# Who makes the low parts of an expert's weights, and where a slot's conversion piece stands

## The chip, the cores and the metric

The kernel runs on one core of a Trainium2 chip. The metric is the device time of one execution in microseconds, lower is better. Three runs of the kernel before gave 1194.30, 1198.21 and 1198.25 us, median 1198.21. The profiled execution took 1196.37 us. Its span, from the first to the last instruction, is 1194.7 us.

TensorE (PE in the views) multiplies matrices, VectorE (DVE), ScalarE (ACT) and GpSimd (POOL) work on elements, SyncE (SP) issues most DMAs.

## What is computed

Three stages stand behind one another. Cut to what matters:

```python
def _moe_ref(x, w_gate, w_output_gate, w1, w2):      # x: 1792 x 768, from attention
    logits = x @ w_gate
    e_idx = np.argmax(logits, axis=1)                # one of 8 experts for each token
    ...
    for e in range(E):
        mask = e_idx == e
        h = np.maximum(x[mask] @ w1[e], 0.0)         # 768 x 1024
        ye = h @ w2[e]                               # 1024 x 768
        out[mask] = gate_w[mask, None] * eom[mask, e, None] * ye

def _moe2_ref(x, w_in, w_out):                       # feed-forward, 768 x 2048 x 768
    h = x @ w_in
    return (h * np.cos(h)) @ w_out
```

Before them an attention with a sigmoid in place of the softmax makes `x` (4 batches, 12 heads, 448 tokens, 64 wide). The feed-forward's weights come as 64-bit floats.

## The kernel before

**High and low parts.** A matmul on full 32-bit floats is done as three matmuls on numbers of a shorter type: each operand is split into a high part (a rounding copy, on ScalarE) and a low part (the number less its high part, on VectorE or GpSimd), and high x high, high x low and low x high are added up in PSUM. The function `split` does this for a piece of weights of 128 x 1536: `w1h` and `w2h` are high parts, `w1l` and `w2l` low parts, four pieces of each for an expert. Its last argument chooses GpSimd for the low part.

**Slots.** The tokens are sorted by expert into slots of 128; here 19 slots (0 to 18) hold tokens. `slot` works on one:

1. `p0`, the left half of the hidden layer: 18 matmuls (`mm1`, lines 242 to 244) with the first two pieces of `w1`. VectorE clips it at zero into `hr` (line 722).
2. `p1`, the right half: 18 matmuls with the last two pieces. After nine of them TensorE turns the left half (`pht`, line 728), ScalarE takes its high part `hh` (line 731), VectorE its low part `hl` (line 732).
3. The next slot's tokens are turned (`xh`, `xl`), and the right half's `hr` is made.
4. The second layer into `py`: eight groups of six matmuls (`mm2`, lines 741 and 742). After the first group the right half is turned; its `hh` and `hl` follow, and seven groups.
5. `scale_y` copies `py`, scaled, to `ysb`, two thirds on ScalarE (line 835) and a third on VectorE (lines 836 and 837), and it is stored.

**A change of expert.** The weights of one expert are in SBUF at a time, and raw weights come into four buffers `rw`. Where slot s+1 has another expert, `split1(s + 1)` at the end of slot s splits the new `w1` and loads the new `w2` into the buffers that this frees. In slot s+1 `split2(0)` to `split2(3)` split `w2` between the slot's own steps, and load the `w1` of the expert after. Which slots have a new expert is known only on the chip, so each split stands in a conditional block on a flag; the engines named in `SPLIT` read the flag. Of `w1l` the fourth piece is GpSimd's; of `w2l` the second is GpSimd's, and of the fourth each of VectorE and GpSimd does half (line 782).

**The conversion piece.** The feed-forward's weights are brought from 64-bit floats to high and low parts in 48 pieces, spread over the whole of the first two stages. `conv_step` does one, and slots 1 to 17 have one each. A piece is: `ctu` on ScalarE, four operations on VectorE, `chi` on ScalarE (which needs VectorE's fourth), a fifth on VectorE, and three on GpSimd (lines 160, 161 and 163). It also stores the piece before and loads the next one.

Each engine works off its instructions in the order in which the code is written; a wait holds up all that stands behind it on that engine.

Of the kernel before, what the change touches and what calls it, by code (L numbers as in the profile page):

```python
# [9 lines left out]
F32 = mybir.dt.float32  # L10
# [5 lines left out]
AF = mybir.ActivationFunctionType  # L16
ALU = mybir.AluOpType
# [3 lines left out]
ENG = mybir.EngineType  # L21
# [3 lines left out]
CONV_EARLY = 40  # L25
# [28 lines left out]
def tile_attn_moe_cos(ctx: ExitStack, tc: tile.TileContext, q, k, v, wg, wog, w1, w2, w_in, w_out, out):  # L54
    nc = tc.nc
# [54 lines left out]
    w1r = [t.rearrange("p (k f) -> p k f", k=3) for t in rw]  # L110
    w2r = [t.rearrange("p (k f) -> p k f", k=2) for t in rw]
# [17 lines left out]
    def conv_load(i):  # L129
        if i >= len(conv_list):  # L130
            return
        which, h, r = conv_list[i]
        raw = craw[i % 2]
        if which == "i":
            src = w_in[r * P : (r + 1) * P, h * CW : (h + 1) * CW].bitcast(U32)
            nc.sync.dma_start(raw.rearrange("p f t -> p (f t)"), src)
        else:
            src = wo_in[h][:, :, r * CO : (r + 1) * CO].bitcast(U32)
            nc.sync.dma_start(raw.rearrange("p (two f) t -> p two (f t)", two=2), src)
# [26 lines left out]
    def conv_store():  # L166
        while conv_out:
            which, h, r, parts_ = conv_out.pop()
            for t, f in enumerate(parts_):
                if which == "i":  # L170
                    c0 = h * CW // P
                    nc.sync.dma_start(
                        wi_d[c0 : c0 + CW // P, :, t, r, :].rearrange("c p f -> p c f"),
                        f.rearrange("p (c f) -> p c f", f=P),
                    )
                else:
                    nc.sync.dma_start(
                        wo_to[h, t][:, :, r * CO : (r + 1) * CO], f.rearrange("p (two f) -> p two f", two=2)
                    )

    conv_at = [0]

    def conv_step(whole=True):
        conv_end()
        conv_store()
        conv_load(conv_at[0] + 1)
        conv_rest.append(conv(conv_at[0]))
        next(conv_rest[0], None)
        conv_at[0] += 1
        if whole:  # L190
            conv_end()
# [3 lines left out]
    def conv_end():  # L195
        while conv_rest:
            next(conv_rest.pop(), None)
# [3 lines left out]
    w1h = [pre.tile([P, 3, 512], F32R, name="w1h0")]  # L201
    w1l = [pre.tile([P, 3, 512], F32R, name="w1l0")]
# [4 lines left out]
    def w1_src_d(e, i):  # L207
        nh, kg = divmod(i, 2)
        return w1[bass.ds(e, 1)].rearrange("o (k p) f -> p (o k) f", p=P)[
            :, 3 * kg : 3 * kg + 3, 512 * nh : 512 * nh + 512  # L210
        ]

    def w2_src_d(e, i):
        return w2[bass.ds(e, 1)].rearrange("o (k p) f -> p (o k) f", p=P)[:, 2 * i : 2 * i + 2, :]

    def split(raw, hi, lo, pool):
        nc.scalar.activation(hi, raw, AF.Copy)  # L217
        (nc.gpsimd if pool else nc.vector).tensor_tensor(lo, raw, hi.bitcast(F32), op=ALU.subtract)  # L218

    def gather(xg, at, rows=NT):  # L220
        nc.gpsimd.indirect_dma_start(
            out=xg,
            out_offset=None,
            in_=x_d[:rows, :],
            in_offset=bass.IndirectOffsetOnAxis(ap=at, axis=0),
        )
# [20 lines left out]
    with ExitStack() as st:  # L247
# [329 lines left out]
        for i in range(n):  # L577
# [8 lines left out]
            elif 6 <= i < 6 + NSLOT - NSURE:  # L586
                s = NSURE + i - 6
# [116 lines left out]
    with ExitStack() as st:  # L704
# [6 lines left out]
        w2h = [wp.tile([P, 2, DM], F32R, name=f"w2h{i}") for i in range(4)]  # L711
        w2l = [wp.tile([P, 2, DM], F32R, name=f"w2l{i}") for i in range(4)]
# [33 lines left out]
        def flag(row, s, engines, top=1):  # L746
            return nc.values_load(fl[0:1, row, s : s + 1], engines=engines, min_val=0, max_val=top)

        SPLIT = [ENG.Activation, ENG.DVE, ENG.Pool]

        def split1(s):
            new = flag(1, s, SPLIT + [ENG.SP])
            e = flag(4, s, [ENG.SP], E - 1)
            for i in range(4):
                with tc.If(new != 0):  # L755
                    split(w1r[i], w1h[i], w1l[i], i == 3)
                    nc.sync.dma_start(w2r[i], w2_src_d(e, i))

        def slot(s, between, when):
            nxt = s + 1 < NSLOT  # L760
            ahead = min(s, 1)
            hh = m2.tile([P, KF, P], F32R, tag="hh", name="hh", bufs=1)
            hl = m2.tile([P, KF, P], F32R, tag="hl", name="hl", bufs=1)
            with when():
                if 0 < s < NSLOT - 2:
                    gather(xgs[s % 2], idx[:, s + 2 : s + 3])
                if s > 1:
                    new = flag(1, s, SPLIT)
                    ld = flag(3, s, [ENG.SP])
                    ne = flag(0, s, [ENG.SP], E - 1)  # L770

                def split2(i):
                    if s == 0:
                        split(w2r[i], w2h[i], w2l[i], i in (0, 2))
                    elif s > 1:
                        with tc.If(new != 0):
                            if i < 3:
                                split(w2r[i], w2h[i], w2l[i], i == 1)
                            else:
                                nc.scalar.activation(w2h[i], w2r[i], AF.Copy)  # L780
                                for j, eng in enumerate((nc.vector, nc.gpsimd)):
                                    eng.tensor_tensor(
                                        w2l[i][:, j], w2r[i][:, j], w2h[i][:, j].bitcast(F32), op=ALU.subtract
                                    )
                        with tc.If(ld != 0):
                            nc.sync.dma_start(w1r[i], w1_src_d(ne, i))

                ph = p0 if s == 0 else ps_h.tile([P, 512], F32, tag="h", name="p0")
                for kc in range(3 if s == 0 else 0, KD):
                    mm1(ph, 0, kc, kc == 0, kc == KD - 1)  # L790
                    between(kc)
                hr0 = relu(ph)
                between("relu")
                split2(0)
                p1 = ps_h.tile([P, 512], F32, tag="h", name="p1")
                for kc in range(KD):
                    mm1(p1, 1, kc, kc == 0, kc == KD - 1)
                    if kc == 2:
                        turn_h(hr0, hh, hl, 0)
                        split2(1)  # L800
                    between(KD + kc)
                hr1 = relu(p1, s <= 1)
                if 0 < s and nxt:
                    turn(xgs[(s + 1) % 2], ps_t, "t")
                if s > 0:
                    split2(2)
                    split2(3)
                py = ps_y.tile([P, 2, 512], F32, tag="y", name="py")
                state["py"] = py
                for kc in range(ahead):  # L810
                    mm2(py, hh, hl, kc)
                    between(2 * KD + kc)
                turn_h(hr1, hh, hl, 1)
                between("h")
                if s == 0:
                    split2(2)
                    split2(3)
            if s >= 1 and conv_at[0] < CONV_EARLY:
                conv_step()
            if nxt and s >= NSURE:  # L820
                split1(s + 1)
            with when():
                for kc in range(ahead, KF):
                    mm2(py, hh, hl, kc)
                    between(2 * KD + kc)
                if s == 0:
                    turn(xgs[1], ps_t, "t")
                elif nxt and s < NSURE:
                    split1(s + 1)
                if s > 0:  # L830
                    scale_y(s)

        def scale_y(s):
            py, ysb = state["py"], ysbs[s % 3]
            nc.scalar.activation(ysb[:, :512], py[:, 0, :], AF.Copy, scale=scs[:, s : s + 1])
            nc.vector.tensor_scalar(ysb[:, 512:DM], py[:, 1, : DM - 512], scs[:, s : s + 1], None, op0=ALU.mult)
            nc.vector.tensor_copy(ysb[:, DM : DM + 1].bitcast(I32), idx0 if s == 0 else idx[:, s : s + 1])
            if s < NSURE:
                store_y(s)
# [194 lines left out]
        def between(s):  # L1034
            def step(k):
                for _ in range(ROUTE_AT.count((s, k))):
                    next(route, None)

            return step
# [263 lines left out]
```

## Time and profile before

| | |
|---|---|
| median of three runs | 1198.21 us |
| profiled execution | 1196.37 us, span 1194.7 us |
| PE busy | 1089.3 us, 91% |
| DVE busy | 778.7 us, 65% |
| ACT busy | 509.0 us, 43% |
| POOL busy | 393.5 us, 33% |

The attention takes the first 260 us of the span, the slots those to 687, the feed-forward the rest. Busy shares are means over these stages. What holds up a slot is read from the rows of the slot: the timeline of an engine gives the start and the duration of an instruction and, in brackets, how long the engine was idle before it and what ended that. The tile views give the number of a tile's instructions with the shortest, the median and the longest duration.

### The profile page before, as it was taken

To read this page: it belongs to the slowest core of one execution; us is meant where nothing else is said; L and a number is where in the kernel's file an instruction comes from. 1 tells how busy PE (TensorE), PEld (TensorE's weight loads), DVE (VectorE), ACT (ScalarE), POOL (GpSimd) and SP (SyncE) were. 2 spreads that over 40 slices of the span, in tenths; PEclk is the share of its full clock that TensorE was granted. 3 is DMA by queue.
4 is the path that set the end of the run, shared out by engine and by line. 5 is a ranking of instruction groups with operands and counts; after the bars stand their busy time and mean duration, and the time that the engine had idled before them with its cause. 6 is when DMAs were issued, how large, how long until landed. Compare 5 with 4: busy or idle time off the path is not lost. (4 is left out here: it accounts for less than half of the span.)

```text
span 1194.7 us, 17366 instructions
## 1 busy us (share of the span) xinstructions
PE 1089.3 (91%) x5740; PEld 870.0 (73%) x5740; DVE 778.7 (65%) x1239; ACT 509.0 (43%) x754; POOL 393.5 (33%) x306
## 2 busy tenths in 40 slices
PE   7899999888998899789789789979999999999997
PEld 5555555546777688568568568858888889999996
DVE  5878887967655844774774648996555555566553
ACT  6666666643242513442542433334323333333332
POOL 4665555372144532663651603440200002001001
PEclk9999999998998999899999989989999999999999
DMA  6778776463538562885784487747665558767751
GB/s 173 197 225 237 222 197 198 143 220 108 209 106 275 182 205 91 268 290 165 254 289 154 134 343 282 270 181 294 217 246 183 188 187 328 264 222 292 262 190 41
DMA packets 118795, 254.72 MB, mean 213 GB/s; under 512 B 9440, under 2 KB 66016, under 8 KB 118688
## 3 DMA queue, kind: packets, MB, share of 16 engines
q1 hardware_dynamic: 114768, 234.19, 57.8%
q0 software_dynamic: 3920, 19.28, 5.0%
q8 instruction: 47, 0.77, 0.3%
q14 instruction: 60, 0.49, 0.1%
HBM read 207.02 MB, written 46.41 MB: 212 GB/s over the span
## 5 line engine op out<-in xcount | busy, mean ns | idle before, releaser
L160 POOL TENSOR_TENSOR ctu<-ctu,cta 128x512 f32<-128x512 f32 x48 | 62.0, 1291 | 325.5 <-DVE cta L157 244.5
L1198 PE MATMUL o<-wo,gh 128*128 128x512 f32 x448 | 168.4, 397 | 0.0
L1222 POOL DMA_INDIRECT out_dram<-osb,at x14 | 14.2, 1011 | 358.8 <-DVE osb L1211 267.5
L1138 PE MATMUL ph<-yh,wi 128*128 128x512 f32 (+1 forms) x318 | 116.3, 366 | 8.2 <-ACT p L1147 5.3
L243 PE MATMUL p<-w1l,xh 128*128 128x512 f32 x228 | 95.1, 417 | 30.5 <-DVE w1l L218 27.9
L1161 ACT ACTIVATE r<-r 128x512 f32<-128x512 f32 (+1 forms) x64 | 37.0, 578 | 188.2 <-DVE r L1156 186.6
L1139 PE MATMUL ph<-yl,wi 128*128 128x512 f32 (+1 forms) x318 | 115.9, 364 | 0.0
L1140 PE MATMUL ph<-yh,wi 128*128 128x512 f32 (+1 forms) x318 | 115.8, 364 | 0.0
L1199 PE MATMUL or<-wo,gh 128*128 128x256 f32 x384 | 108.3, 282 | 0.0
L242 PE MATMUL p<-w1h,xh 128*128 128x512 f32 x228 | 95.7, 420 | 4.9 <-ACTq L755 2.7
L1198 PEld LDWEIGHTS o<-wo,gh 128*128 128x128 f32 x448 | 84.1, 188 | 17.5 <-ACT gh L1171 0.4
L312 ACT ACTIVATE aT<-sc,b_sig 112x896 f32<-112x896 f32 x96 | 91.4, 1004 | 6.7 <-PE sc L309 6.4
L244 PE MATMUL p<-w1h,xl 128*128 128x512 f32 x228 | 92.9, 407 | 0.0
L1198 PE MATMUL o<-wo,gl 128*128 128x512 f32 x224 | 88.4, 395 | 0.7 <-DVE gl L1172 0.7
L316 PE MATMUL av<-aT,v 112*64 112x448 f32 x384 | 84.5, 563 | 0.0
L1167 DVE TENSOR_TENSOR r<-r,p 128x512 f32<-128x512 f32 (+1 forms) x64 | 39.9, 624 | 66.0 <-ACT r L1162 66.0
L309 PE MATMUL sc<-T,kl 128*112 128x448 f32 x192 | 73.1, 381 | 9.9 <-DVE kl L288 9.8
L218 DVE TENSOR_TENSOR w1l<-rw,w1h 128x1536 fp32r<-128x1536 f32 x22 | 72.3, 3336 | 14.0 <-ACT w1h L217 8.8
L243 PEld LDWEIGHTS p<-w1l,xh 128*128 128x128 f32 x228 | 45.1, 198 | 46.4 <-DVE w1l L218 35.7
L309 PE MATMUL sc<-T,kh 128*112 128x448 f32 x192 | 75.7, 394 | 2.3 <-ACT kh L286 1.6
L1152 DVE TENSOR_SCALAR t<-p 128x512 f32<-128x512 f32 (+1 forms) x64 | 33.8, 528 | 65.8 <-ACT p L1147 65.8
L731 ACT ACTIVATE hh<-pht 128x512 fp32r<-128x512 f32 x38 | 22.6, 595 | 119.0 <-PE pht L728 119.0
(259 smaller groups left out, 2807.7 us busy)
## 6 DMA issues: line engine op xcount, KB each, us to landing
rw<-in_moe_w_dram SPq DMA_DIRECT2D x64, 768.0 KB, 6.0
wo<-wo_d SPq DMA_DIRECT2D x64, 768.0 KB, 4.5
wi<-wi_d SPq DMA_DIRECT2D x53, 768.0 KB, 5.9
craw<-in_moe_w_in_dram SPq DMA_DIRECT2D x25, 512.0 KB, 5.3
craw<-in_moe_w_out_dram SPq DMA_DIRECT2D x24, 512.0 KB, 4.8
er<-wi_d SPq DMA_DIRECT2D x11, 768.0 KB, 6.6
ys_d<-ysb SPq DMA_DIRECT2D x19, 384.5 KB, 3.8
wi_d<-chi SPq DMA_DIRECT2D x24, 256.0 KB, 3.3
```

The lines of the kernel that those rows point to most:

```text
L218: (nc.gpsimd if pool else nc.vector).tensor_tensor(lo, raw, hi.bitcast(F32), op=ALU.subtract)
L242: nc.tensor.matmul(ps, xh[:, kc], wh, start=first, stop=False)
L243: nc.tensor.matmul(ps, xh[:, kc], wl, start=False, stop=False)
L244: nc.tensor.matmul(ps, xl[:, kc], wh, start=False, stop=last)
L309: nc.tensor.matmul(ps[:, j, :S], kk[j][part][:, c * CP : (c + 1) * CP], T[j], start=s, stop=not s)
L312: nc.scalar.activation(aT[:, c], ps[:, :, :S], AF.Sigmoid, bias=b_sig[:CP], scale=1.0 / math.sqrt(D))
L316: nc.tensor.matmul(pav[D * j : D * j + D, :S], t["v"][:, j, c, :], aT[:, c, j], start=c == 0, stop=c == NC - 1)
L1138: nc.tensor.matmul(ph[:, :w], wih[:, kc], yh[:, kc, :w], start=kc == 0, stop=False)
L1139: nc.tensor.matmul(ph[:, :w], wih[:, kc], yl[:, kc, :w], start=False, stop=False)
L1140: nc.tensor.matmul(ph[:, :w], wil[:, kc], yh[:, kc, :w], start=False, stop=kc == KD - 1)
L1198: nc.tensor.matmul(acc[i], g[:, ts_], w[:, :512], start=f, stop=l)
L1199: nc.tensor.matmul(acc["r", i], g[:, ts_], w[:, 512:], start=f and (own or i % 2 == 0), stop=l, skip_group_check=True,)
```

## The change

VectorE makes all low parts of a new expert's weights; GpSimd makes none, and no longer reads the flag. The conversion piece of a slot is issued after the slot's `scale_y`, where it stood between the second `hl` and `split1`. Slot 0's splits stay as they are.

```diff
-        SPLIT = [ENG.Activation, ENG.DVE, ENG.Pool]
+        SPLIT = [ENG.Activation, ENG.DVE]
 
         def split1(s):
...
             for i in range(4):
                 with tc.If(new != 0):
-                    split(w1r[i], w1h[i], w1l[i], i == 3)
+                    split(w1r[i], w1h[i], w1l[i], False)
                     nc.sync.dma_start(w2r[i], w2_src_d(e, i))
...
                     elif s > 1:
                         with tc.If(new != 0):
-                            if i < 3:
-                                split(w2r[i], w2h[i], w2l[i], i == 1)
-                            else:
-                                nc.scalar.activation(w2h[i], w2r[i], AF.Copy)
-                                for j, eng in enumerate((nc.vector, nc.gpsimd)):
-                                    eng.tensor_tensor(
-                                        w2l[i][:, j], w2r[i][:, j], w2h[i][:, j].bitcast(F32), op=ALU.subtract
-                                    )
+                            split(w2r[i], w2h[i], w2l[i], False)
...
-            if s >= 1 and conv_at[0] < CONV_EARLY:
-                conv_step()
             if nxt and s >= NSURE:
                 split1(s + 1)
             with when():
...
                 if s > 0:
                     scale_y(s)
+            if s >= 1 and conv_at[0] < CONV_EARLY:
+                conv_step()
```

On VectorE, from the last step of a slot to the first of the next, before (the piece writes `cta` and `ctf`; `w1l` are the low parts, `ysb` the result, `hr` the next slot's first step; lines of a branch left out):

```order
L732 TENSOR_TENSOR hl<-pht,hh 128x512
L152 TENSOR_SCALAR cta<-craw_101 128x512
L153 SCALAR_TENSOR_TENSOR ctf<-craw_101,cta 128x512
L154 TENSOR_SCALAR cta<-craw_101 128x512
L155 SCALAR_TENSOR_TENSOR ctf<-cta,ctf 128x512
L157 TENSOR_SCALAR cta<-ctf 128x512
...
L218 TENSOR_TENSOR w1l_2752<-rw_96,w1h_2749 128x1536
...
L218 TENSOR_TENSOR w1l_2753<-rw_97,w1h_2750 128x1536
...
L836 TENSOR_SCALAR ysb_2766<-py,scs 128x256
L837 COPY ysb_2766<-idx 128x1
```

And now, from the last two `w1l` on:

```order
L218 TENSOR_TENSOR w1l_2753<-rw_97,w1h_2750 128x1536
...
L218 TENSOR_TENSOR w1l_2754<-rw_98,w1h_2751 128x1536
...
L829 TENSOR_SCALAR ysb_2764<-py,scs 128x256
L830 COPY ysb_2764<-idx 128x1
L152 TENSOR_SCALAR cta<-craw_100 128x512
L153 SCALAR_TENSOR_TENSOR ctf<-craw_100,cta 128x512
L154 TENSOR_SCALAR cta<-craw_100 128x512
L155 SCALAR_TENSOR_TENSOR ctf<-cta,ctf 128x512
L157 TENSOR_SCALAR cta<-ctf 128x512
L747 TENSOR_LOAD fl
L722 TENSOR_SCALAR hr<-p_4440 128x512
```

The piece moved from ahead of the `w1l` to between `ysb` and `hr`, and a fourth `w1l` came in.

On ScalarE at the same place, before (`w1h` the high parts, `ctu` and `chi` the piece's):

```order
L731 ACTIVATE hh<-pht 128x512
L151 ACTIVATE ctu<-craw_101 128x512
L159 ACTIVATE chi<-ctf 128x512
L747 TENSOR_LOAD fl
L755 COMPARE_AND_BRANCH
L217 ACTIVATE w1h_105<-rw_95 128x1536
```

And now:

```order
L217 ACTIVATE w1h_2751<-rw_98 128x1536
L755 UNCONDITIONAL_BRANCH x2
L828 ACTIVATE ysb_2766<-py,scs 128x512
L151 ACTIVATE ctu<-craw_100 128x512
L159 ACTIVATE chi<-ctf 128x512
L747 TENSOR_LOAD fl
L747 ISA x2
L776 COMPARE_AND_BRANCH
L217 ACTIVATE w2h_2755<-rw_95 128x1536
```

`chi`, which waits for VectorE, stood ahead of the first `w1h` and stands ahead of the first `w2h`.

On VectorE within a slot, the steps around the second `split2`, before:

```order
L732 TENSOR_TENSOR hl<-pht,hh 128x512
L776 COMPARE_AND_BRANCH
L776 UNCONDITIONAL_BRANCH x2
L785 UNCONDITIONAL_BRANCH
L722 TENSOR_SCALAR hr<-p_4017 128x512
```

And now:

```order
L732 TENSOR_TENSOR hl<-pht,hh 128x512
L776 COMPARE_AND_BRANCH
L218 TENSOR_TENSOR w2l_2760<-rw_96,w2h_2756 128x1536
L776 UNCONDITIONAL_BRANCH x2
L778 UNCONDITIONAL_BRANCH
L722 TENSOR_SCALAR hr<-p_4466 128x512
```

The second `w2l` came in between `hl` and the slot's second `hr`.

## Rows read from the trace of the kernel before

**Rows 1.** The page, busy time, share of the span and instructions by engine

```profile
PE 1089.3 (91%) x5740; PEld 870.0 (73%) x5740; DVE 778.7 (65%) x1239; ACT 509.0 (43%) x754; POOL 393.5 (33%) x306
```

**Rows 2.** ScalarE's timeline, `ysb` of five slots (start, duration, idle before, releaser)

```profile
310.80 0.69 ACT L835 ACTIVATE ysb<-py,scs 128x512 f32<-128x512 f32 x1 [2.99 <-PE py L742]
...
333.19 0.69 ACT L835 ACTIVATE ysb<-py,scs 128x512 f32<-128x512 f32 x1 [2.98 <-PE py L742]
...
441.23 0.69 ACT L835 ACTIVATE ysb<-py,scs 128x512 f32<-128x512 f32 x1 [2.60 <-PE py L742]
...
459.34 0.69 ACT L835 ACTIVATE ysb<-py,scs 128x512 f32<-128x512 f32 x1 [2.98 <-PE py L742]
...
685.84 0.69 ACT L835 ACTIVATE ysb<-py,scs 128x512 f32<-128x512 f32 x1 [4.94 <-PE py L742]
```

**Rows 3.** Tile view of w1l: duration ns min/median/max; who waited, us, times

```profile
L218 DVE TENSOR_TENSOR w1l<-rw,w1h x22: 1746/2846/5049, 267.7 to 664.0; 128x1536 fp32r<-128x1536 f32 x22
...
  PE p L243: 27.9, 20
```

**Rows 4.** TensorE's timeline: slot 2's start, the first change

```profile
313.54 0.79 PE L243 MATMUL p<-w1l,xh 128*128 128x512 f32 x1 [2.54 <-DVEq L755]
...
351.10 0.39 PE L242 MATMUL p<-w1h,xh 128*128 128x512 f32 x1
...
360.22 0.50 PE L243 MATMUL p<-w1l,xh 128*128 128x512 f32 x1 [2.62 <-DVE w1l L218]
...
374.64 0.80 PE L741 MATMUL py<-w2h,hl 128*128 128x512 f32 x1 [2.04 <-DVE hl L732]
```

**Rows 5.** ScalarE's timeline before the first change

```profile
344.01 0.60 ACT L731 ACTIVATE hh<-pht 128x512 fp32r<-128x512 f32 x1 [0.84 <-PE pht L728]
...
347.69 0.63 ACT L159 ACTIVATE chi<-ctf 128x512 fp32r<-128x512 f32 x1 [2.52 <-DVE ctf L155]
348.28 5.61 ACT L217 ACTIVATE w1h<-rw 128x1536 fp32r<-128x1536 f32 x4
```

**Rows 6.** VectorE's timeline: the first change, then an ordinary slot

```profile
349.80 10.37 DVE L218 TENSOR_TENSOR w1l<-rw,w1h 128x1536 fp32r<-128x1536 f32 x3 [1.68 <-ACT w1h L217]
...
367.55 1.02 DVE L235 TENSOR_TENSOR xl<-pxt,xh 128x512 fp32r<-128x512 f32 x2 [0.38 <-ACT xh L234]
...
453.29 0.42 DVE L152 TENSOR_SCALAR cta<-craw 128x512 uint32<-128x512 uint32 x1
...
455.73 0.43 DVE L157 TENSOR_SCALAR cta<-ctf 128x512 uint32<-128x512 uint32 x1
460.07 0.48 DVE L836 TENSOR_SCALAR ysb<-py,scs 128x256 f32<-128x256 f32 x1 [3.92 <-ACT ysb L835]
...
463.45 0.69 DVE L722 TENSOR_SCALAR hr<-p 128x512 f32<-128x512 f32 x1 [2.84 <-PE p L244]
```

**Rows 7.** Tile view of w2l: GpSimd's half pieces, count, duration ns

```profile
L782 POOL TENSOR_TENSOR w2l<-rw,w2h x7: 2053/2608/2613, 371.0 to 680.5; 128x768 fp32r<-128x768 f32 x7
```

**Rows 8.** GpSimd's timeline: the first change, and two changes in a row

```profile
349.54 1.30 POOL L161 TENSOR_TENSOR ctf<-ctf,chi 128x512 f32<-128x512 f32 x1
...
353.97 4.59 POOL L218 TENSOR_TENSOR w1l<-rw,w1h 128x1536 fp32r<-128x1536 f32 x1 [0.37 <-ACT w1h L217]
...
496.79 2.44 POOL L782 TENSOR_TENSOR w2l<-rw,w2h 128x768 fp32r<-128x768 f32 x1 [0.87 <-ACT w2h L780]
...
526.12 2.61 POOL L782 TENSOR_TENSOR w2l<-rw,w2h 128x768 fp32r<-128x768 f32 x1 [2.40 <-ACT w2h L780]
```

**Rows 9.** Stretches: length, then busy PE, PEld, DVE, ACT, POOL, clock, DMA, GB/s

```profile
366.00:372.30 6.30, 6.30 (x39) 5.41 (x39) 4.82 (x5) 5.06 (x7) 4.83 (x2) 1.00 0.88 323
374.64:378.00 3.36, 3.36 (x10) 2.87 (x11) 2.52 (x5) 0.63 (x1) 0.49 (x1) 0.50 0.84 291
```

**Rows 10.** DMA issues: size of one, median us from issue to landing

```profile
rw<-in_moe_w_dram SPq DMA_DIRECT2D x64, 768.0 KB, 6.0
```

**Rows 11.** VectorE's timeline, the end of the routing in slot 1

```profile
312.12 0.17 DVE L1030 TENSOR_TENSOR gidx<-gr,rank 128x14 int32<-128x14 f32 x1
```

## The prediction

> **What bounds the kernel now.** I read the page's part on busy time first: TensorE computes for 91% of the span [rows 1], so a gain must come out of the stretches in which it doesn't. The change touches the expert stage alone, so I next paced that stage by the copy of a slot's result, `ysb`, which ScalarE starts as soon as TensorE has ended the slot [rows 2]. An undisturbed slot takes 459.34 - 441.23 = 18.11 us. Slots 1 to 18 (18 such copies, 17 steps) take 685.84 - 310.80 = 375.0 us, and 17 x 18.11 = 307.9 us; so 67.1 us are lost in the stage. The step from slot 1 to 2 takes 22.39 us and loses 4.3 of them. The other 62.8 lie at the seven slots where a new expert begins (seven halves of `w2l` on GpSimd [rows 7]), 9.0 us each. The rows of slots 9 to 11 and of 14 and 15 show that four of the seven come in pairs of neighbouring slots: GpSimd's half follows after 29.3 us at 496.79 and 526.12 [rows 8].
>
> The tile view of `w1l` says what ends TensorE's waits there: VectorE's low parts, 27.9 us in 20 waits on matmuls alone [rows 3]. At the first change TensorE starts the slot at 351.10, is stopped before 360.22 for 2.62 us by a `w1l`, and before 374.64 for 2.04 us by an `hl`, an eviction queued on VectorE behind low parts [rows 4]. After such a wait the granted clock is 0.50 (1.2 GHz) for 3.36 us, after 1.00 just before [rows 9], so a wait of 2 us costs about 1.7 more.
>
> Why `w1l` is late: three of them take VectorE 10.37 us from 349.80 [rows 6], while the shortest takes 1.75 [rows 3]. Over the same time GpSimd runs the conversion piece and the fourth low part, which takes 4.59 us [rows 8]. And the first starts only when `w1h` does, at 348.28, because ScalarE waited 2.52 us for the piece's VectorE part before `chi` [rows 5].
>
> **The change, part by part.** I count from 0, the start of the second `hh` of the slot before (344.01), and take an isolated change.
>
> *ScalarE.* `ctu` and `chi` no longer stand ahead of `w1h`. It starts 0.5 after `hh` instead of at 348.28 - 344.01 = 4.3, and its four copies end at 6.1 (5.61 for four [rows 5]). The raw weights have long landed: they were loaded a change earlier.
>
> *VectorE's four `w1l`.* The first starts 1.5 after `w1h` (as now: 349.80 - 348.28), at 2.0. GpSimd has no elementwise work left there, so I take the shortest duration, 1.75, for all four: they end at 9.0. TensorE enters the slot at 7.1 (351.10), needs the first then and the third 4.1 us later; all are there. The waits at `w1l` go.
>
> *What is late next: the piece, then `hr0`.* `ysb` on ScalarE follows at 7.3 and takes 0.69; VectorE's part takes 0.54 (463.45 less the idle 2.84 less 460.07) and ends at 9.5. The piece's five operations take 455.73 + 0.43 - 453.29 = 2.9 [rows 6]: 12.4. `hr0` takes 0.69: 13.1. TensorE wants it 27 matmuls into the slot; 18 of them take 463.45 - 459.34 = 4.1, so at 7.1 + 6.2 = 13.3. Just in time. In an undisturbed slot the same piece fits the 2.84 us in which VectorE now idles before `hr0` [rows 6], and another 1.4 us are spare before TensorE needs it: cost 0 there, and up to 1 us a slot if that cover were gone.
>
> *The four `w2l`.* `chi` now stands ahead of `w2h` on ScalarE and is released at 12.0, so the first `w2h` is ready at 14.1. GpSimd now runs the piece from 12.5, three operations of 1.3 [rows 8]. I let the first `w2l` wait 0.9 for the second of these, and the second 0.6 for the third: 1.5 us of meetings. First `w2l` to 16.8, `hl` (an eviction like `hr`, 0.7) to 17.4, second `w2l`, which GpSimd did until now, to 19.8, the second `hr` to 20.4, `xl` 1.02 to 21.4, two more `w2l` (3.5) to 24.9, the second `hl` to 25.6. Half of the slot's last seven groups of matmuls (7.1 us) is still to come: TensorE ends at 29.1. Undisturbed it would at 7.1 + 18.1 = 25.2. So the excess is 3.9, and 4.2 with part of a clock drop, since TensorE waits 2.6 us for the second `hr`. This is VectorE's bound: its work in the slot adds up to some 21 us against 18.1.
>
> The Trainium skill (SBUF — State Buffer, Who interferes with whom) has the two engines share a port pair as an exclusive lock, so that a VectorE operation with two SBUF inputs and a GpSimd operation that reads SBUF block each other for a whole instruction. The pairs of 10.37 and 4.59 against 1.75 for one [rows 3, 6, 8] agree. By that rule the 1.5 us of meetings stay in the sum; if the two only shared bandwidth, they would shrink, and the whole would come out some 8 us faster.
>
> Bounds of the excess: 2.4 with no meeting and no clock drop, 5.5 if two more low parts meet a GpSimd operation of 1.3. I take 4.2.
>
> *The second of a pair.* Its `w1` is loaded into the buffers that the first change's `w2l` free; the last is free at 24.9, lands 6.0 later [rows 10], and goes through `w1h` (1.4) and `w1l` (1.75) to 34.3. With `ysb` (0.54) and the piece, `hr0` comes at 38.4. TensorE, in the slot since 29.3, wants it at 35.5: 2.9 us late. From `hr0` the chain above runs again, 16.2 us, to 54.6, where 29.3 + 18.1 = 47.4 would be undisturbed. Excess 7.2, bounds 5 and 9.
>
> *Slot 1.* TensorE's wait before 313.54 ends when VectorE has passed the skipped splits [rows 4], behind `gidx`, which ends at 312.29 [rows 11]. With the piece out of the way this comes 2.9 earlier and the 2.54 us of wait go, with the half clock behind them: of 4.3 lost I keep 0.5, so 3.8 gained (bounds 2 and 4.3).
>
> *Other queues.* GpSimd loses the conditional blocks and issues the gather after the piece, some 6 us later; the gathered rows are used a slot (18 us) after. On SP the piece's stores and next load come behind the store of `ysb`; the load of 5 us is wanted a whole slot later. Cost 0; were the load late, the piece and so `hr0` would move with it.
>
> *Sum.* Seven changes now 62.8; then 3 x 4.2 + 2 x (4.2 + 7.2) = 35.4; gain 27.4, with slot 1 31.2. Low bound of the gain: 5 x 5.5 + 2 x 9 = 45.5, 17.3 + 2 = 19. High: 5 x 2.4 + 2 x 5 = 22, 40.8 + 4.3 = 45. The profiled execution took 1196.4 (span 1194.7 and 1.7 around it): 1196.4 - 31.2 = 1165.2. The median shown lies 1.8 above the profiled one; I predict 1166.
>
> **Rivals.**
> - *VectorE hides more.* No meetings, and the evictions slip in without stopping TensorE: the high bound, 1196.4 - 45 = 1151. For it: in an ordinary slot VectorE idles 2.84 us before `hr0` alone [rows 6], so a backlog is soon paid. Against: in the change slot itself `hr` and `hl` stand in line behind low parts.
> - *Half of the gain.* The second `hr` behind the second `w2l` stops TensorE longer, the clock drops at every change as now, and a pair costs 9: the low bound and some, 1180. For it: two waits of over 2 us and a half clock at the first change today [rows 4, 9].
> - *VectorE becomes the bound outright, slower.* One mechanism: the low parts don't go back to 1.75 because something other than GpSimd stretches them (ScalarE writing `w1h`, the weights' DMAs). There are 7 x 8 = 56 of them in the chain before TensorE's end; 31.2 / 56 = 0.56, so beyond 1.75 + 0.56 = 2.3 us on average the change loses. At the present median of `w1l`, 2.85 [rows 3], it would lose 56 x 1.1 - 31 = 30: 1227. Against: GpSimd's low part lies over just the 10.37 us that are stretched [rows 6, 8].
> - *No effect.* The piece delays `hr0` in each of some ten ordinary slots past its spare 1.4 us, by another 3 us: 1195. Its room of 2.84 speaks against.
>
> **How the numbers follow.** Forecast 0.62 (its own range 1156 to 1175), more hidden 0.14, half 0.14, no effect 0.04, slower 0.06. About 0.5%, 6 us, is what a measurement of this kernel can tell from no change. Faster by more than that: 0.62 + 0.14 + 0.14 = 0.90; same 0.04; slower 0.06. The range from 1149 to 1184 takes in both bounds of the costs and leaves out the last two cases and the ends of the others.
>
> **What would show it.** Right: `w1l` near 1.75 us at each change; no matmul ended by `w1l` except perhaps in the pairs; TensorE's waits moved to `hr` or `hl` of the change slot, behind `w2l`; slot 1 to 2 at 18 to 19 us; isolated changes near 22 us, the second of a pair near 25; ordinary slots still 18.1 with no idle VectorE time before `hr0`. Wrong: `w1l` over 2.3 us, `hr0` late in ordinary slots, or `chi` holding the first `w2h` so long that TensorE waits for `w2l`.

## The result and the profile after

The changed kernel takes 1164.88 us (median of four runs, 1162.44 to 1166.19) against 1196.26 before: 31.4 us less, ratio 0.9737 with a 95% interval of 0.9706 to 0.9768. The prediction was 1166. The profiled span went from 1194.7 to 1160.7 us.

The pace of the slots after, by ScalarE's `ysb` (the same columns as [rows 2]; the operation now has line 828):

```profile
308.53 0.69 ACT L828 ACTIVATE ysb<-py,scs 128x512 f32<-128x512 f32 x1 [6.70 <-PE py L742]
326.64 0.69 ACT L828 ACTIVATE ysb<-py,scs 128x512 f32<-128x512 f32 x1 [6.70 <-PE py L742]
...
423.65 0.69 ACT L828 ACTIVATE ysb<-py,scs 128x512 f32<-128x512 f32 x1 [6.70 <-PE py L742]
441.77 0.69 ACT L828 ACTIVATE ysb<-py,scs 128x512 f32<-128x512 f32 x1 [6.70 <-PE py L742]
...
650.79 0.69 ACT L828 ACTIVATE ysb<-py,scs 128x512 f32<-128x512 f32 x1 [8.27 <-PE py L742]
```

An ordinary slot takes 18.1 us as before. Slots 1 to 18 take 650.79 - 308.53 = 342.3 us, 34.4 more than 17 x 18.11, where before they lost 67.2 [rows 2]. So 32.8 us of the 34.0 by which the span is shorter were gained between these two rows. The other 1.2 are outside the changed code: the first row comes 2.3 us earlier, and from the last one to the end it takes 1.1 longer. That first row stood anywhere from 308.4 to 311.7 in the runs below, with no pattern, so I count it as noise. Between the two slots of a pair `ysb` doesn't give TensorE's pace: it stands on ScalarE behind `w1h`, which waits there for raw weights (in the first pair it started at 484.43, and TensorE's last matmul ended at 480.96).

The tile view of `w1l` answers to [rows 3]: no matmul waits for it any more (one weight load does, 0.3 us), and the longest of VectorE's takes what the shortest took.

```profile
L218 DVE TENSOR_TENSOR w1l<-rw,w1h x29: 1743/1753/1759, 266.8 to 627.7; 128x1536 fp32r<-128x1536 f32 x29
...
  DVE hr L722: 3.8, 6
  PEld p L243: 0.3, 1
```

The first change, all engines but TensorE in order of time (answers to [rows 5, 6, 8]):

```profile
338.27 5.62 ACT L217 ACTIVATE w1h<-rw 128x1536 fp32r<-128x1536 f32 x4 [0.21 <-ACT hh L731]
339.80 6.77 DVE L218 TENSOR_TENSOR w1l<-rw,w1h 128x1536 fp32r<-128x1536 f32 x4 [1.01 <-ACT w1h L217]
...
349.37 0.64 ACT L159 ACTIVATE chi<-ctf 128x512 fp32r<-128x512 f32 x1 [3.36 <-DVE ctf L155]
...
350.58 0.69 DVE L722 TENSOR_SCALAR hr<-p 128x512 f32<-128x512 f32 x1 [0.78 <-issue]
...
352.32 1.77 DVE L218 TENSOR_TENSOR w2l<-rw,w2h 128x1536 fp32r<-128x1536 f32 x1 [1.05 <-ACT w2h L217]
352.55 2.69 POOL L163 TENSOR_TENSOR clo<-ctu,ctf 128x512 fp32r<-128x512 f32 x1
...
354.61 2.24 DVE L218 TENSOR_TENSOR w2l<-rw,w2h 128x1536 fp32r<-128x1536 f32 x1
...
356.78 0.68 DVE L722 TENSOR_SCALAR hr<-p 128x512 f32<-128x512 f32 x1
```

Four `w1l` take 6.77 us where three took 10.37, and start behind `hh`, not behind the piece. TensorE's waits (answers to [rows 4]) are now in front of `pht`, for `hr`: 21.8 us in 12 waits over slots 2 to 18. At the first change:

```profile
351.33 0.66 PE L728 MATMUL pht<-ident,hr 128*128 128x128 f32 x4 [0.47 <-DVE hr L722]
357.51 0.66 PE L728 MATMUL pht<-ident,hr 128*128 128x128 f32 x4 [1.77 <-DVE hr L722]
362.37 0.50 PE L741 MATMUL py<-w2h,hl 128*128 128x512 f32 x1 [0.39 <-DVEq L755]
```

and in the second slot of each pair:

```profile
490.44 0.65 PE L728 MATMUL pht<-ident,hr 128*128 128x128 f32 x4 [3.33 <-DVE hr L722]
...
575.68 1.12 PE L728 MATMUL pht<-ident,hr 128*128 128x128 f32 x4 [5.29 <-DVE hr L722]
```

### The profile page after: what moved, and what is told of

The parts are those of the page before. It is cut to its first block, busy times and chain, and to the rows that moved or that the text cites. A ratio compares the mean times of both kernels' runs of the same rounds, so it can differ in the third digit from the quotient of the medians.

```text
span 1160.7 us, 16962 instructions
## 1 busy us (share of the span) xinstructions
PE 1075.7 (93%) x5740; PEld 865.4 (75%) x5740; DVE 762.2 (66%) x1253; ACT 509.4 (44%) x754; POOL 318.5 (27%) x285
## 5 line engine op out<-in xcount | busy, mean ns | idle before, releaser
L242 PE MATMUL p<-w1h,xh 128*128 128x512 f32 x228 | 93.0, 408 | 0.5 <-ACT xh L234 0.5
L243 PE MATMUL p<-w1l,xh 128*128 128x512 f32 x228 | 90.4, 397 | 0.0
L244 PE MATMUL p<-w1h,xl 128*128 128x512 f32 x228 | 90.4, 397 | 0.0
L1131 PEld LDWEIGHTS ph<-yh,wi 128*128 128x128 f32 x318 | 60.4, 190 | 16.9 <-ACT p L1140 5.7
L1192 PEld LDWEIGHTS or<-wo,gh 128*128 128x128 f32 x384 | 72.4, 189 | 0.7
L1165 DVE TENSOR_TENSOR gl<-r,gh 128x512 fp32r<-128x512 f32 (+1 forms) x64 | 46.8, 731 | 38.9 <-ACT gh L1164 38.9
```

Source lines behind the costliest of these rows:

```text
L242: nc.tensor.matmul(ps, xh[:, kc], wh, start=first, stop=False)
L243: nc.tensor.matmul(ps, xh[:, kc], wl, start=False, stop=False)
L244: nc.tensor.matmul(ps, xl[:, kc], wh, start=False, stop=last)
L1131: nc.tensor.matmul(ph[:, :w], wih[:, kc], yh[:, kc, :w], start=kc == 0, stop=False)
L1192: nc.tensor.matmul(acc["r", i], g[:, ts_], w[:, 512:], start=f and (own or i % 2 == 0), stop=l, skip_group_check=True,)
```

## The experiments

The theory: GpSimd's operations that read SBUF and VectorE's that do so hold each other up, so VectorE's low parts are late; and the piece ahead of `w1h` makes them later. The main rival: the place of the piece did it all, or VectorE, now with all low parts, is simply near its limit and the order of its queue doesn't matter. For each run I took its time, and the loss in the stage: the start of `ysb` in slot 18 less that in slot 1 less 307.9 us. The loss comes from one profiled execution: a second profile of each of the last two kernels gave 25.7 and 23.3 in place of 27.1 and 19.2, so it doesn't tell differences of under 4 us apart.

| kernel | us | ratio to before, interval | first and last `ysb` | lost |
|---|---|---|---|---|
| before | 1196.2 | 1 | 310.80, 685.84 | 67.2 |
| the change | 1164.9 | 0.9737, 0.9706 to 0.9768 | 308.53, 650.79 | 34.4 |
| engine only | 1169.5 | 0.9772, 0.9728 to 0.9816 | 308.92, 658.91 | 42.1 |
| place only | 1186.1 | 0.9905, 0.9868 to 0.9941 | 308.98, 674.91 | 58.1 |
| `w1l` on VectorE, `w2l` shared | 1178.1 | 0.9841, 0.9798 to 0.9885 | 310.79, 666.68 | 48.0 |
| the change, no pieces in slots | - | - | 311.08, 632.99 | 14.0 |
| before, no pieces in slots | - | - | 310.62, 642.80 | 24.3 |
| the change and junk that reads | 1175.9 | 0.9830, 0.9795 to 0.9864 | 310.61, 662.68 | 44.2 |
| the change and junk that writes | 1165.2 | 0.9740, 0.9705 to 0.9775 | 309.02, 651.21 | 34.3 |
| `hr` first | 1156.8 | 0.9661, 0.9636 to 0.9686 | 310.27, 645.22 | 27.1 |
| `hr` first, piece in the middle | 1150.3 | 0.9609, 0.9593 to 0.9625 | 311.72, 638.76 | 19.2 |

**The two halves of the change.** The changed kernel with the piece at its old place:

```diff
+            if s >= 1 and conv_at[0] < CONV_EARLY:
+                conv_step()
             if nxt and s >= NSURE:
                 split1(s + 1)
...
                 if s > 0:
                     scale_y(s)
-            if s >= 1 and conv_at[0] < CONV_EARLY:
-                conv_step()
```

> VectorE makes all low parts of a changed expert, the conversion piece stays ahead of split1. Theory (both parts are needed: the meetings with GpSimd and the late start of w1h): w1h starts 4.3 us after hh as before, the first two w1l meet the piece's GpSimd operations, TensorE waits about 1.2 and 0.9 us at w1l and 0.8 at hr0; 5 us lost at an isolated change, 12 at a pair, 4.3 again from slot 1 to 2: 45 us lost in the stage against 34.4 after the change, about 1175 us. Rival, the engine alone matters: 1165 us and no wait at w1l. Rival, the place alone matters: 1195 us.

1169.5 us; 26.7 of the 31.4 us without moving the piece. TensorE's waits in it:

```profile
311.58 0.68 PE L243 MATMUL p<-w1l,xh 128*128 128x512 f32 x1 [2.48 <-DVEq L755]
...
350.71 0.50 PE L243 MATMUL p<-w1l,xh 128*128 128x512 f32 x1 [1.01 <-DVE w1l L218]
```

The wait before slot 2 is back (its 2.54 before, none after), and 1.0 us at the first `w1l` of a change. The loss of 42.1 was expected at 45; the time lies midway between the theory's 1175 and the 1165 of "the engine alone".

The kernel before with only the piece moved (that diff the other way round, in the kernel before):

> GpSimd keeps its share of the low parts, only the piece moves behind scale_y. Theory (both parts are needed): w1h starts early, but GpSimd's w1l still stretches one of VectorE's, and its second w2l comes behind the piece's three operations and the gather, so that TensorE waits for w2l in the second layer: about 1175 us. Rival, the place alone matters: VectorE has 4.4 us less to do in a change slot than in the changed kernel, so 1160 us or less. Rival, the engine alone matters: 1192 us, slot 1 to 2 at 18.1 us in every case.

1186.1 us, 10.2 less than before and far from the 1160 that the place alone would have given. My own theory had 1175; the time is nearer to the 1192 of "the engine alone". Slot 1 to 2 takes 18.1 us (308.98 to 327.09), so that part is the place's. What then holds it up, in GpSimd's and VectorE's timelines at the first change:

```profile
358.03 3.46 POOL L218 TENSOR_TENSOR w2l<-rw,w2h 128x1536 fp32r<-128x1536 f32 x1
361.44 1.84 POOL L782 TENSOR_TENSOR w2l<-rw,w2h 128x768 fp32r<-128x768 f32 x1
```

```profile
346.39 2.60 DVE L152 TENSOR_SCALAR cta<-craw 128x512 uint32<-128x512 uint32 x1
...
358.31 6.59 DVE L218 TENSOR_TENSOR w2l<-rw,w2h 128x1536 fp32r<-128x1536 f32 x1 [0.46 <-ACT w2h L217]
```

VectorE's `w2l` starts 0.3 us behind GpSimd's and ends at 364.9, 1.6 us after the second of GpSimd's two: if it stood still through both, the 1.6 are about its 1.75 alone. The piece's first operation, 0.42 elsewhere, takes 2.60 beside GpSimd's `w1l`. I had expected that `w1l` to stretch one of VectorE's; it stretches none, all 22 take 1.74 to 1.76. Over these slots TensorE waits 20.2 us for `hr`, 7.6 for GpSimd's `w2l` and 2.7 for VectorE's.

**Less work for VectorE, not less time.** The change, but with `w2l` shared as before (in the place-only kernel):

```diff
-                    split(w1r[i], w1h[i], w1l[i], i == 3)
+                    split(w1r[i], w1h[i], w1l[i], False)
```

> The piece moved and w1l all on VectorE, but w2l shared with GpSimd as before (the second piece and half of the fourth). If VectorE's sum of work bounds the change slot: 2.6 us less of it, 1150 to 1158 us. If meetings decide: GpSimd's second w2l stands behind the piece's operations and meets VectorE's third, 1165 to 1172 us, TensorE waiting at w2l.

1178.1 us: 13 us slower than the change, with 2.6 us less for VectorE to do at each change. So VectorE's sum of work is not what bounds a change. The time lies above both ranges. TensorE's waits at `w2l` (total, times, longest):

```profile
PE py L741 <- POOL w2l L218: 12.3, 5, 2.5
...
PE py L741 <- DVE w2l L218: 4.3, 4, 1.1
```

Most is waiting for GpSimd's own second `w2l`, which stands behind the piece's operations and takes 3.45 us for VectorE's 1.75. VectorE's third `w2l` beside it took up to 7.13. So both count here, the meetings and GpSimd's own lateness, and this run doesn't part them.

**The meeting by itself.** The change, with work on GpSimd that nobody waits for, in `split1`'s block (GpSimd reads the flag again for it; `junk_view` is `junk` as 128 x 2 x 128):

```diff
                     split(w1r[i], w1h[i], w1l[i], False)
+                    nc.gpsimd.tensor_copy(junk[:, :1], w1h[i][:, 0, :1].bitcast(F32))
+                    for j in range(2):
+                        nc.gpsimd.tensor_tensor(junk_view, ident2, ident2, op=ALU.subtract)
```

> The changed kernel with GpSimd work that nobody waits for beside each w1l of a changed expert: a copy of one element a row behind w1h, and two subtractions of 128x256 that read SBUF twice. If the two engines hold each other up when both read SBUF (the Trainium skill, SBUF - State Buffer, Who interferes with whom): w1l goes from a median of 1.75 us to 2.3 or more, with no wait for data added, TensorE waits at w1l or hr0 again, and 5 to 15 us come back: 1170 to 1180 us. If GpSimd's share was slow for its own speed and place in line only: w1l stays at 1.75 and the time within 3 us of 1165.

And with `nc.gpsimd.memset(junk, 0.0)` as the last line:

> As the run before, with two memsets of 128x256 in place of the subtractions, so that GpSimd only writes (besides the copy of one element a row). By the reading of both engines: w1l stays at 1.75 us, 1163 to 1168 us. If any GpSimd work at all slows VectorE down: w1l as in the run before.

1175.9 and 1165.2 us. With reads, the tile views of `w1l` and of the junk, then VectorE at the first change:

```profile
L218 DVE TENSOR_TENSOR w1l<-rw,w1h x29: 1751/1825/2172, 267.7 to 638.7; 128x1536 fp32r<-128x1536 f32 x29
```

```profile
L761 POOL TENSOR_TENSOR junk<-ident x56: 612/676/2017, 343.8 to 645.9; 128x256 f32<-128x256 f32 x56
```

```profile
341.92 7.60 DVE L218 TENSOR_TENSOR w1l<-rw,w1h 128x1536 fp32r<-128x1536 f32 x4 [1.05 <-ACT w1h L217]
...
349.90 0.64 DVE L152 TENSOR_SCALAR cta<-craw 128x512 uint32<-128x512 uint32 x1
350.65 0.92 DVE L153 SCALAR_TENSOR_TENSOR ctf<-craw,cta 128x512 uint32<-128x512 uint32 x1
```

With memsets, VectorE at the same place and the junk:

```profile
340.32 6.77 DVE L218 TENSOR_TENSOR w1l<-rw,w1h 128x1536 fp32r<-128x1536 f32 x4 [1.05 <-ACT w1h L217]
```

```profile
L761 POOL MEMSET junk<- x56: 310/312/569, 342.2 to 631.2; 128x256 f32 x56
L759 POOL COPY junk<-w1h x28: 684/866/1772, 340.4 to 629.9; 128x1 f32<-128x1 f32 x28
```

Reads on GpSimd that no instruction depends on cost 11 us; memsets in their place cost nothing that can be measured, and the four `w1l` take 6.77 us as in the change. With memsets GpSimd reads the flag again too, so no longer reading it was worth nothing that can be measured. The Trainium skill (SBUF — State Buffer, Who interferes with whom) has only a GpSimd operation that reads SBUF contend with a VectorE operation with two SBUF inputs; these two runs agree. A memset is also shorter than a subtraction (0.31 us against 0.68), but six of them lie within the four `w1l` of the first change and stretch none.

The size was off: `w1l` rose to a median of 1.83 us only, not 2.3, because in many meetings GpSimd's operation was the one to wait (a subtraction of 0.68 took up to 2.02); it ran late and met the piece as well. At the first change the four `w1l` took 0.83 us more and the piece's five operations 1.0 more, and `hr` behind them came later. Over slots 2 to 18 TensorE's waits for `hr` grew from 21.8 us to

```profile
PE pht L730 <- DVE hr L724: 30.3, 14, 5.8
```

and the loss by 9.8. With memsets the waits are 21.8 too.

**Without pieces.** `CONV_EARLY = 23` leaves no piece in slots 1 to 17; they are made in the feed-forward, which makes the whole longer (1249.3 and 1259.9 us in one run each) and is not the question; ordinary slots take 18.1 us there as elsewhere. In the changed kernel:

> The changed kernel with no conversion piece in slots 1 to 17 (they are all made in the feed-forward, so only the pace of the slots counts, not the time of the whole). If the piece ahead of hr0 is what makes the second slot of a pair late: the waits of 3.3 and 5.3 us before pht there go to under 1, and the 34.4 us lost over slots 1 to 18 fall to 20 to 25; the wait for the second hr in each change slot stays at 1.7 to 2.2. If the raw weights' DMAs make the pair late, the waits stay within 1 us of what they are and 30 us or more are lost.

And in the kernel before:

> The kernel before, with GpSimd's share of the low parts, but no conversion piece in slots 1 to 17 (only the pace of the slots counts, as in the run of the changed kernel without pieces, which lost 14.0 us over slots 1 to 18). If GpSimd's share alone holds VectorE up: 22 to 35 us lost, w2l of VectorE up to 3.5 to 6 us. If it needs the piece's operations in front of GpSimd's share to make it late: 10 to 15 us lost.

14.0 and 24.3 us lost. So a piece in each slot costs the changed kernel 20.4 us in the stage, more than the 9 to 14 that I expected, and before the first `pht` the second slots of the pairs wait 0.67 us instead of 3.33 and 1.26 instead of 5.29:

```profile
563.26 0.66 PE L728 MATMUL pht<-ident,hr 128*128 128x128 f32 x4 [1.26 <-DVE hr L722]
```

The waits for the second `hr` fell to 0.7 to 0.9 too, which I had expected to stay. In the kernel before, 24.3 lies in the range of "GpSimd's share alone", though VectorE's `w2l` took 3.0 us at most at a change, not 3.5 to 6. GpSimd's share costs 10.3 us even with no piece (24.3 - 14.0), and 24 to 25 with it (67.2 - 42.1 and 58.1 - 34.4): so some 14 us of what the change of engine is worth come only where GpSimd's share and the piece are both there.

**The order in VectorE's queue.** The change, with the second `w2l` behind the second `hr`, and the last behind the second `hl`:

```diff
                         turn_h(hr0, hh, hl, 0)
-                        split2(1)
+                        if s == 0:
+                            split2(1)
...
                 hr1 = relu(p1, s <= 1)
+                if s > 0:
+                    split2(1)
...
                     split2(2)
-                    split2(3)
...
                 turn_h(hr1, hh, hl, 1)
...
                 if s == 0:
                     split2(2)
-                    split2(3)
+                split2(3)
```

> The changed kernel, with the second w2l behind the slot's second hr and the last w2l behind the second hl, on VectorE and ScalarE. If TensorE's loss in a change slot is the place of hr in VectorE's queue (waits of 1.7 to 2.2 us at pht in all seven changes): these go, with some of the half clock, 1 us may come back at w2l; 8 to 12 us less, 1153 to 1157 us. Rival, VectorE's sum of work in the slot (some 21 us against 18.1) is the bound whatever its order: 1162 to 1165 us, the waits moved to w2l or to the next hr0.

1157.8 us (median of four runs), the waits for the second `hr` gone. The order matters. The largest waits left are for the first `hr` of a pair's second slot, in TensorE's timeline:

```profile
488.89 1.11 PE L728 MATMUL pht<-ident,hr 128*128 128x128 f32 x4 [4.49 <-DVE hr L722]
```

Built on it, the piece in the middle of `split1`, with all `w1h` ahead of it:

```diff
-            for i in range(4):
-                with tc.If(new != 0):
-                    split(w1r[i], w1h[i], w1l[i], False)
-                    nc.sync.dma_start(w2r[i], w2_src_d(e, i))
+            for i in range(4):
+                with tc.If(new != 0):
+                    nc.scalar.activation(w1h[i], w1r[i], AF.Copy)
+                    if i < 2:
+                        low1(i, e)
+            if piece:
+                conv_step()
+            for i in (2, 3):
+                with tc.If(new != 0):
+                    low1(i, e)
...
                 if s > 0:
                     scale_y(s)
-            if s >= 1 and conv_at[0] < CONV_EARLY:
-                conv_step()
```

`low1` is VectorE's low part and the load of `w2`; `piece` says whether the slot has a piece.

> Built on the kernel with hr first (1157.8 us): the piece now stands between the second and the third w1l on VectorE, with all four w1h ahead of it on ScalarE. If in a pair VectorE waits for the raw weights there (0.6 and 1.3 us before w1l) while the piece behind them holds up hr0: the pairs lose 2 to 3 us less each, the waits of 4.5 and 5.2 us shrink to 2, isolated changes within 1 us of what they are: 1151 to 1155 us. Rival, the piece's GpSimd operations now meet the last two w1l and stretch them by 1.3 each, and VectorE's sum stays the bound: 1157 to 1162 us.

1152.7 us (median of four runs). The difference of the two lay inside their intervals, so both ran again side by side:

> The kernel with hr first and the piece between the second and the third w1l again, for its interval: 0.960 to 0.966 of the time before, below the changed kernel's 0.9706 to 0.9768.

> The kernel with hr first alone again, beside the run before it on one chip: if the place of the piece is worth its 2 to 4 us on top, 0.966 to 0.969; if not, the two are the same within 1.5 us.

1150.3 and 1156.8 us; the intervals no longer meet. In the second slot of the first pair VectorE now reads:

```profile
480.41 1.76 DVE L767 TENSOR_TENSOR w1l<-rw,w1h 128x1536 fp32r<-128x1536 f32 x1 [1.35 <-ACT w1h L757]
482.09 0.42 DVE L152 TENSOR_SCALAR cta<-craw 128x512 uint32<-128x512 uint32 x1
...
484.87 4.51 DVE L767 TENSOR_TENSOR w1l<-rw,w1h 128x1536 fp32r<-128x1536 f32 x2
...
489.76 0.67 DVE L722 TENSOR_SCALAR hr<-p 128x512 f32<-128x512 f32 x1
490.36 1.76 DVE L218 TENSOR_TENSOR w2l<-rw,w2h 128x1536 fp32r<-128x1536 f32 x1
```

With `hr` first alone it reads:

```profile
482.22 1.76 DVE L218 TENSOR_TENSOR w1l<-rw,w1h 128x1536 fp32r<-128x1536 f32 x1 [0.22 <-ACT w1h L217]
484.23 1.76 DVE L218 TENSOR_TENSOR w1l<-rw,w1h 128x1536 fp32r<-128x1536 f32 x1 [0.25 <-ACT w1h L217]
...
490.28 0.69 DVE L722 TENSOR_SCALAR hr<-p 128x512 f32<-128x512 f32 x1 [1.06 <-issue]
492.09 2.75 DVE L218 TENSOR_TENSOR w2l<-rw,w2h 128x1536 fp32r<-128x1536 f32 x1 [1.12 <-ACT w2h L217]
```

The piece takes the place of waits for `w1h` that were only 0.22 and 0.25 us here, and the two `w1l` behind it take 4.51 us, 1.0 more than alone, since they meet its GpSimd operations. What is seen to go is the idle time before `hr` and before the first `w2l`, and that `w2l`'s stretch. Which of these gives the gain stays open. In these two profiles the second slots of the pairs, by TensorE's last matmul, take 24.4 and 24.5 us with the piece in the middle and 27.7 and 26.0 without; in the profiles of the first runs of the same two kernels they take 26.9 and 26.2 with it and 26.2 and 26.1 without. So the time came out as expected, but that the pairs lose 2 to 3 us less was seen in one profile of two. At 1150.3 us this version beats both kernels, by 47.0 us against before (1197.3 in these runs).

## Why the prediction was right

*`w1l` without GpSimd, 1.75 us each.* Right: 1.74 to 1.76 in all 29. The four end 9.1 us after `hh`; 9.0 were forecast.

*The piece, then `hr0`, just in time.* Nearly: `hr0` ends 0.7 us later than I worked out, since VectorE stands idle for 0.78 us before it, where it reads the flag, with no releaser that the profile shows, and TensorE waits 0.47 us. In ordinary slots nothing was lost, as forecast.

*The meetings that stay, 1.5 us.* Mis-sized: at the first change the first `w2l` took 1.77 us and lost nothing, since GpSimd's `clo` was the one to wait (2.69 us); the second took 2.24. So 0.5 in place of 1.5, and the first `w2l` came 1.05 us late for another reason, `chi` ahead of `w2h`, which the working had.

*The excess of an isolated change.* Forecast 4.2 us; from the `ysb` rows it is 3.3 and 3.2 for the first two, and 5.0 for the last. At the first change TensorE's wait for the second `hr` was 1.8, not 2.6. The granted clock was 1.00 over the whole of the first two slots, so there was no clock drop for the 0.3 that I had put in; over the last it was 0.93 on average.

*The pairs.* Forecast 11.4 each, 4.2 and 7.2; measured 9.8 and 13.1; taken from TensorE's last matmul of one slot to that of the next, 3.0 and 6.8 in the first pair, 3.9 and 9.2 in the second. One sum was off: 24.9 + 6.0 + 1.4 + 1.75 is 34.05 and not 34.3, which takes 0.25 us from each pair. The wait at the second slot's `hr0` was to be 2.9 us and was 3.3 and 5.3. The run without pieces, where 0.67 and 1.26 are left, shows what the piece adds; that `w1h` waits for the raw weights' landing ahead of it, ScalarE's rows show in the first pair:

```profile
477.92 1.50 ACT L217 ACTIVATE w1h<-rw 128x1536 fp32r<-128x1536 f32 x1 [1.50 <-DMA rw<-in_moe_w_dram]
481.03 1.49 ACT L217 ACTIVATE w1h<-rw 128x1536 fp32r<-128x1536 f32 x1 [1.61 <-DMA rw<-in_moe_w_dram]
```

In the later pair 1.43 us of the wait are idle time of VectorE before `hr` with no releaser, which stays open, and the half clock came back: 0.50 (1.2 GHz) over the 4.4 us behind the wait. The second slots, and that stretch, with the columns of [rows 9]:

```profile
481.00:505.90 24.90, 19.03 (x99) 15.38 (x98) 17.97 (x20) 12.31 (x13) 7.55 (x4) 1.00 0.95 324
564.10:591.40 27.30, 21.15 (x99) 17.23 (x99) 18.19 (x20) 12.31 (x13) 5.98 (x4) 0.87 0.89 313
575.60:580.00 4.40, 4.32 (x12) 3.57 (x13) 3.19 (x4) 3.18 (x3) 4.03 (x3) 0.50 0.68 266
```

*Slot 1.* Forecast a gain of 3.8; the 4.3 went whole, and only where the piece was moved or left out.

*The sum.* Loss forecast 35.4 and 0.5, measured 34.4. That it came so near is in part luck: terms of 1 us were off in both directions.

*What I had not separated.* The working gave the early start of `w1h` and the end of the meetings as if one gain. The runs give 26.7 us to the engine and 10.2 to the place, each alone, and 31.4 together. So most of the gain doesn't need both, as my theory for the first two runs had it. Behind the change of engine, moving the piece is worth 4.6 by the times, whose intervals overlap, and 7.7 by the loss; slot 1 to 2 gives 4.4 of it. And calling the remaining loss "VectorE's bound" was wrong: with the same work in another order 14.6 us of the time went, 8.0 of them with `hr` first alone.

## What to carry to other kernels

Work handed from a busy VectorE to GpSimd isn't free when both read SBUF: here taking it back, more work for the busier engine, made the kernel 2.3% faster. Sum up an engine's work, but look at the order of its queue before calling it the bound: a low part that is needed late must not stand ahead of an eviction that TensorE needs now. And try other places for a piece of background work: here the piece in the middle of `split1` was worth another 6.5 us, though which of its effects did it isn't shown.

## What the runs showed of the hardware

VectorE's blocked operation got no turn between two GpSimd operations that followed closely: 6.59 us for 1.75, through 3.46 and 1.84. In the run with `w2l` shared it took 7.13 though it had started 0.26 us ahead of GpSimd's 3.45 (358.42 against 358.68); why is not shown. And GpSimd's copy of one element a row, 0.26 us at its shortest in the run with subtractions, took up to 1.77 beside a `w1l`, while memsets beside one went on at 0.31: the read is what is held up.
